# A new order table for the fused attention and MoE kernel, and other numbers of attention units per token chunk

## The chip, the cores and the metric

The kernel runs on one core of one Trainium2 chip. Its time is the device time of one execution in microseconds, the median of several runs. The core has five instruction queues: TensorE (PE in the profile, with its weight loads as PEld), VectorE (DVE), ScalarE (ACT), GpSimd (POOL) and SyncE (SP). In this kernel POOL and SP carry no arithmetic worth speaking of: POOL issues the loads from memory, SP issues the stores and the transposes by DMA.

## The reference

Sliding-window attention with a distance bias, then a two-layer MoE block with a cosine gate:

```python
# q, k, v: (8, 8, 576, 64)
scores = scale * q @ k^T
bias = slopes[:, None, None] * (-np.abs(rel))
mask = (rel >= 0) & (rel < 128)
scores = np.where(mask, scores + bias, -1e9)
attn = softmax(scores)
x = (attn @ v).transpose(0, 2, 1, 3).reshape(4608, 512)
h = x @ w_in             # (4608, 2048)
g = h * np.cos(h)
out = g @ w_out          # (4608, 512)
```

## The kernel before

**Attention.** A batch has nine *units*: for each half of its first 512 tokens (`G` = 0, 1) four pairs of heads, and one tail unit `t` with the last 64 tokens of all heads. Units are taken two at a time. Each pair goes through a chain that changes engine at every step:

- `scores` (PE, L497, the tail L488): keys times queries into four PSUM banks. These matmuls use 64 rows of the array, all others 128.
- `exps` (ACT, L529, tail L521), then `mask` (DVE, L553, tail L540), which multiplies by the precomputed bias and window `emask`.
- `pv` (PE, L584 and L587, tail L571 and L573): probabilities times `vp`; a column of ones in `vp` gives the sum.
- `norm` (DVE, L623 and L625, tail L610 and L613): reciprocal and product. Where the two units of a pair are neighbours of the same half and the count of units so far is even, `norm_two` (L638 and L640) does both at once.
- The result is turned into `xT`, either by PE (`x_pe`, L691, copied by L700 on ACT or L701 on DVE; `x_pe_two`, L653 and L664), or by a DMA transpose that SP issues (`x_dma`, L714, tail L709) where there is time.

**MoE.** Tokens are cut into nine chunks of 512. `moe1` (chunk 0: `moe1_half`, L753, L758, L762) makes 16 *feature blocks* per chunk: four matmuls of L729 into one bank, the cosine on ACT (L735), the product `gT` on DVE (L739). The bank comes free when DVE has finished. `moe2` multiplies `gT` with `w_out`: plainly for chunk 0 (`moe2_plain`, L814, L820, L826), and for the others with seven products of Strassen's scheme (L870), sums made by DVE (`g_sums`, L804), reads by ACT (L890) and DVE (L894), stores by SP (L915).

**Which units stand beside which chunk.** Batch 0 is done ahead of the loop. Beside chunk `c` stand the next `QUOTA[c]` units (L272, used in L1018). Their chain fills the waiting times of MoE work and the other way round.

**Loads.** POOL issues, in program order: the pieces of q and k for batches 0 and 1 (L309), the weights `w_inb` (L360) and `w_outb` (L366), `vp` by `load_v` (L328, five per batch, two buffers by `b % 2`), and from batch 2 on q and k in natural layout by `load_nat` (L338). `load_v` reads the key `("vinit", b % 2)`: it waits for DVE's memsets of that buffer (L393 and L394). From batch 2 on SP transposes q and k by DMA (`dma_transposes`, L349 and L352) into `qt` and `kt`, which `scores` reads.

**Order.** `Plan.op` records every step with what it reads and writes. `Plan.schedule` does not search: it decodes the string `STARTS` into a 16-bit number for every step. The upper 15 bits are a start number, the lowest bit picks DVE or ACT for steps that may run on either. Steps are sorted by start number, and each engine gets its own steps in that order:

```python
            code = (code + 256 * raw[i] + raw[n + i]) & 0xFFFF
            o.start = code >> 1
            if len(o.eng) > 1:
                e = "dve" if code & 1 else "act"
...
        self.order = sorted(self.all, key=lambda o: (o.start, o.seq))
```

The start numbers themselves are not on the chip. `Plan.emit` puts semaphore waits where a step's data or buffer comes from another engine or from a DMA; a queue is strictly in order, so a step that waits holds all steps behind it on its engine. POOL's steps keep program order whatever the table says.

Of the kernel before, what the change touches and what calls it, by code (L numbers as in the profile page):

```python
# [14 lines left out]
B, H, S, D = 8, 8, 576, 64  # L15
# [12 lines left out]


STARTS = (  # L30
    "c-p;I4^&iD8lM5w+uPIjylD=XA&1L@)!DZ=!DE==&YKwm#u0JCBtYD7mURWuZ3#Cu{8JK=x<ux>u7#<cUH{g))KN}(j+SLb="
    "&I{6D{HsS&X)FPv&{tL&+K<+U>Fz>t8@09^WNP1-S7VSe&6r+-O*@$J(|9!uhpaVX*8odd>UV%3k|Km<KwSJ)7K1nq9P)@uL"
    "MRknm(tV{xt&zU!Oy8d|+1#zgn%PBkV-Mg-2{@hOqVA;CeSY+8we<r#3R^(-%g6-xty!7_)ESnr;5xs7Or&$3W9QI>M*DJUF"
    "6J?Sm~*or4UKn!!HWknQ_6^o4}c9byUh8SdLN7<OL>NWr!*1iFC%kGd8(ZkP5doDeea>(UOJzpw=KJ`p`5x`eMXx@|B(+Hg>"
    "MIBx#7HZ<FVvo@k7gc-hpx){V5txwxOldEkY-2NYa&WNtixxhZZTs7J@f1UwF&38sI{0VdE%~mMS!YrsG3`JiMzoAgP5nO#k"
    "(ait$1Pzf<SA%D03nsW1?$Mgip0=kmq8G6CfK}W5-O-5b8qp<8mzvR6ud{G}fL%kD8*O;u8Dj1a8r2R>m|j{!x_!Ovi0+V*&"
    "Y>977BX#g=eMJ{GP|$!7M@P+|A&x6#OE7I*4H8A^+h~P-P80FGJp^?BZAo<!)X@KY%c{PB0ECojryjShh5(Tgw7FN#)RD%H("
    "lu~dy##n&LM@X`3}PE9wr;17a{*fb#?b^xL<mmP=lcp+4eoO*gY~2dTzkd5mNR;Gab-g;M)_%fMG1!fd4?o@DR1yjuAr)OKQ"
    "}}A!={n-qTzi=HP*#`wo7+5H;7e0Jr(c!Y*ZB@Vvt--8V#3K5b`6yb=Dt3E^w_hOy;M@O?gkO4R>cPESlU=x$H{P;S@lYI2t"
    "Ddc^H^y4`h^$)7~kAHigf?{cxWO;@zz8OO%wzjivEwsiP_hugiz*6faRmFXwn{zy%nn*4_0(Fa%7I;FYtM|3y2H%&S#PM`j4"  # L40
    "aRgoZS2}mDLpqBy5?-Ek$o61k>B?DFv0b_)=_)O#IC|x$tCwtxzb_H#5fac^^-lu)ib7H?dr3eTA&i|Y7Ev=n0x=afA}=47^"
    "lZF<L~xaLES4aN&(*837-kTJ2zwM!FSLj`b1|5N1JbLdQ;!OKOh7tz(7&=E61EcwZYt!~>K=%}9)xXtv{2;3m6GoLGDScxO5"
    "{m1;v5NE7LLs~dvoWVp6`9(MC)=Q>hH)9FM484Ul{k#Z{2AY$*iB@tN9(XJ|`vn)_#>cI}L(NB_G5+tIYE?6gtF<%2=WyFG|"
    "1KbXVFqns9=Hc<G(d4d=YPHTK}o6TKU#OT^Wpl&%!u+eC~FmU>)+MWsZPptlQ)PWrIPDfZB<ISLld*p1I+B_^N6L@#0yJ4>*"
    "rrw58RxbvwZO6=FzB~n(1vALc-w7!}e*xq9o*5^3V<huX9sQ!W$87WIqJk-S2;bqEm>OEAUiRuE*4aZOB!<RiFiG;FKN)4W*"
    "9<8Eck~&_bGG&W5o8vua^$$&vGAAFD&3}>C&tIIK&Jt2qHE(a7V-+0<>ymTcYB-gK)r60vxALYyz%vCN<}%BcwSTvmkDRyYv"
    "mSGjN)M8G!V&-IE+-2Wi04obZ?ayAUKbogL=WjC?ybD1mwSx@ihYphmougoC8AYGm}tGghp1jaOOTw1>hf6XQvz~=EeZUJIL"
    "+2=F95tKJBURI0>j(zddHK-eNjrr-@J=(3457r!<*SH7~6^*zr$iVRUK5yDp2Dw#Yw7KMMM)TGrF*aO{bU`?rGdgFlCRI5F2"
    "Hyxev=e-SUj_kXd~Ict0cNXi}?e9-C7{=B5BA64FnSx{W)g8^>~n+(aVCwx*gNEqmMA+mlT>sU+9<a+)H&<4vHfRyN14*O?Q"
    "5UBzEo_8)TBx(}?-c^kb-i6y;6v-~qsX(yF3M+C!5jujwOArMRg7$wKOg@P~=&=X2bUICb;3*tDx=s*e+8~vk+V!3RVP?3P5"  # L50
    "?>GX2;wu)@9Y`LxLRhZdh>@9tE#;c{(o*WgL%0`3Y+$?LTd&T>`Bet>%VdgAI%ek=U^Dv|?D>v|M64+6BOtMveF_NO$^Hly%"
    "2Htko4Ot7ouux@P>?bngVazq26RBx<xiQ_+|x@_oGo|%o-F%7$w}M1J;U8@zhgzc**()#IWt9kx;_m{OV1fCH@7yJKjc;Coq"
    "5GZOIp)8vN{bU_nP+$3bc!=ZuLI@>K0SEWkW@LkW+z=&Hxy=poJ;W%!7pJ!#FS~1D+BuDd(F4=(;%3cr)g8?or^8?0g;=vNO"
    ";4nTb#lTHAoARJHQ$0wg6TfwcjXq`Eg0Dcbr83RE5glpv#o2u753V~d}{_3U+V$qG!}r|nPg-0YM96YxtA@&t<9l7YP@LX}f"
    "&pvSpz1{rD@WeWgMqfD@2>0U$yqdy&UAr8KWtnS4|B9~(^ku~zIU=KrPp>RNeVOT{?szP8h(#&jyvjWz0WN)iHwIkE2oE06e"
    "^DCOSpIG`!`hr+?q`{PP7x}0DJu8;1mnY)!cB3=(Wci*sQ$)S^aqFHl?h3c7c(*r;<GX+MIG3&3BNBlGP$c_Y=|U|D;w{E}C"
    "4{B`3%4gf>~CT?rGFNh_!5T%Rbr_1z&gPa9r+(*@=qW*Ij1#$3re-Zv9nA_vY|U6ym@lslhy_R4J4>=3QdzmslM#ZL(Mp!t+"
    "c<3J&wjnM9ez86lmtLE=a~8-$q_z*&0qf_8WdBvT2G7gx*%fS2*aW<s}i98`yh(&*@t%H|L6FDeG5Rb{b0BS2Z7RPH{lZ{dE"
    "7kN={7as>l>Nxl7eaR-0_TzxD<4_)KM=F}6}NTE_qOPCMiDbUd~4T1&1z-E{5i0W1WZfQL4yY=m<JqQcP!1E_GZAqjBN-IwG"
    "in;lpPWs;zA(U0@KOsWXM0xtm>$31*GjP<$r908WhTX4(WVi7RhLgc*W5`hXh+FC(5Q)W;XmeqAoyXx8Wrc&I+RxdKv)v1dW"  # L60
    "C69t|jV?fiDlS9gH*o#rs8cAlORSATft$M6WmBru$&^ZlsW*85z!`7a0KbJk!tb1!7n`>?zvMWRc%<y)DkW#l>DMxN=q`_R@"
    "5A>4iDqSc8x~boUD$W&{6!)m*~qib8LE3VP>^_d$VN>lW~#us+l!Jc6LR+^4v~>8A%r;j#UH&|Ksms7<U)3G&0cL>XuU#+M}"
    "{7%GQtm%qpf@73uG&)LY1(S;u5M;tuUR`&zPW)&6JhNn>>bDPudAE;Oh&;GR>awuXElCHLitvC#h>hSGALUD^aD1sT*4Wi8;"
    "&6HpB4;yq;y0EtCPLF~>y{Xf&m!N|6c=*X(yCF~z&-jMH*V+AYW)MC2BQQ=14Sq+CGWEU#TOKUeh`AvS&V^EH2l_$VzRHU%Q"
    "Xx|6bG<Pztoh#2?~x3U1@hssQlELKZ0er(z+e%4UIFI{+JthWhN){Bx~IG`jU+M0LXm9;CAmBYQxrqS|(MaSQ#MO!J0%-U+8"
    "RwyW+(YT|usm8$m0b4h)y_HG<EsMp9r}XeCdjTXelI+Jxj`0PrxD1ZM0_vepWVo=AX8*xM?FRL<w{}tW7SoR}QP3$4FqNOGC"
    "2uVz<P#T0&LVF`E0$?W-mMZ`1Q-|D6`ov0Z=@%b1A(-{faI-!W~6SGl2=h*wWoFigk3LdXlHzP{4p5jbL+V`k#Kav`w69h2G"
    "mEi$A6&-=+^ju$Nvukga^0"
)


# [150 lines left out]
def bass_alibi_sliding__then__act_gcu_kernel(  # L222
# [8 lines left out]
    with ExitStack() as ctx:  # L231
        def sb(name, shape, dt=BF16):
            return ctx.enter_context(nc.sbuf_tensor(name, shape, dt))

        R = Plan(nc, ctx)
# [8 lines left out]
        T = {n: sb(f"wsum{n}", [128, HF, 256], F16) for n in (1, 2, 3, 4)}  # L244
# [9 lines left out]
        P = [sb(f"p{i}", [128, 2, 512]) for i in range(NP)]  # L254
# [14 lines left out]

        ps = ctx.enter_context(nc.psum_tensor("ps", [128, 8, 512], F32))  # L270
        BPE = 2
        QUOTA = [9, 9, 12, 10, 8, 10, 5]  # L272
        SB, UB, OB = [4, 5, 6, 7], [2, 3], [0, 1]

        slopes = [2.0 ** (-8.0 * (h + 1) / H) for h in range(H)]
# [508 lines left out]
        NG = 2  # L784
# [220 lines left out]
        for c in range(NCH):  # L1005
# [8 lines left out]
            else:  # L1014
                for fc in range(NFC):
                    moe1(c, fc, (UB + SB)[fc % 6] if done < len(every) else
                         (UB + SB)[(16 * c + fc) % 6])
            n = QUOTA[c] if c < len(QUOTA) else 0  # L1018
            attention(every[done:done + n], c)
# [40 lines left out]
```

The softmax here doesn't subtract the row's maximum and nothing guards it: scores larger than these inputs give would overflow.

## Time and profile before

| | |
|---|---|
| median of 4 runs | 305.56 us (305.48 to 305.7) |
| the profiled execution | 305.43 us, of which the span of instructions is 303.7 us |
| PE busy | 293.9 us, 97% of the span |
| DVE, ACT, POOL busy | 252.0 us (83%), 203.9 us (67%), 94.9 us (31%) |
| mean granted TensorE clock | 0.994 of full speed |
| MoE1 matmuls (L729), busy | 125.9 us |
| MoE2 products (L870), four groups, busy | 46.8, 46.1, 43.7 and 26.3 us |
| loads by POOL, median from issue to landing | `qnat` 9.0, `knat` 13.1, `w_outb` 21.4, `vp` 7.7 us |
| transposes by SP, median to landing | `qt` 6.9, `kt` 8.5 us |

A line of the waits says who waited for whom: engine, tile and line, then the total in us, the number of times and the longest. A line of the timeline has the start and the length in us, the engine, the line, the operation, the tile written and read, the number of instructions, and in brackets the idle time ahead and what ended it. Matmuls are pipelined: a record runs from a matmul's start to the end of its last result, so the records of matmuls that follow one another overlap.

### The profile page before, as it was taken

To read this page: it belongs to the slowest core of one execution; us is meant where nothing else is said; L and a number is where in the kernel's file an instruction comes from. 1 tells how busy PE (TensorE), PEld (TensorE's weight loads), DVE (VectorE), ACT (ScalarE), POOL (GpSimd) and SP (SyncE) were. 2 spreads that over 40 slices of the span, in tenths; PEclk is the share of its full clock that TensorE was granted. 3 is DMA by queue.
4 is the path that set the end of the run, shared out by engine and by line. 5 is a ranking of instruction groups with operands and counts; after the bars stand their busy time and mean duration, and the time that the engine had idled before them with its cause. 6 is when DMAs were issued, how large, how long until landed. Compare 5 with 4: busy or idle time off the path is not lost.

```text
span 303.7 us, 7149 instructions
## 1 busy us (share of the span) xinstructions
PE 293.9 (97%) x2893; PEld 197.7 (65%) x2911; DVE 252.0 (83%) x542; ACT 203.9 (67%) x293; POOL 94.9 (31%) x122
## 2 busy tenths in 40 slices
PE   8699999998999999999999999999999999999996
PEld 3478745546874587537888886468646765555785
DVE  3788758789888998989988988999988976788963
ACT  6796877688556787797757875778667935556211
POOL 7998240053998701860188004000000000000000
PEclk9889999999999999999999999999999999999999
DMA  7999999999999999999899989960120314010044
GB/s 144 181 203 210 207 164 155 131 190 123 163 192 156 156 173 178 149 162 165 101 166 149 165 108 108 174 136 15 25 69 4 95 28 143 14 35 0 2 139 140
DMA packets 148353, 38.09 MB, mean 125 GB/s; under 512 B 133984, under 2 KB 147040, under 8 KB 148320
## 3 DMA queue, kind: packets, MB, share of 16 engines
q0 software_dynamic: 99344, 18.10, 80.0%
q1 hardware_dynamic: 48976, 19.54, 33.3%
q8 instruction: 23, 0.38, 0.5%
q14 instruction: 10, 0.08, 0.1%
HBM read 36.70 MB, written 9.44 MB: 152 GB/s over the span
## 4 chain that ended last, share of the span: by engine, by line
PE 89%; DMA 4%; DVE 3%; SPq 2%; ACT 1%; issue 1%; DVEq 0%
PE ps L870 32%; PE ps L729 32%; PE ps L497 5%; PE ps L814 5%; PE ps L753 5%; PE ps L584 3%; DMA kt<-knat 2%; PE ps L587 2%; SPq L349 2%; PE ps L442 1%; DMA ob<-in_q_dram 1%; PE ps L691 1%; PE ps L488 1%; DVE p L553 1%; PE ps L571 1%
## 5 line engine op out<-in xcount | busy, mean ns | idle before, releaser
L729 PE MATMUL ps<-xT,w_inb 128*128 128x512 bf16 (+1 forms) x558 | 125.9, 355 | 0.9 <-issue 0.2
L735 ACT ACTIVATE cos<-ps,halfpi 128x512 f32<-128x512 f32 x128 | 83.0, 686 | 46.1 <-PE ps L729 33.0
L739 DVE TENSOR_TENSOR gT<-ps,cos 128x512 f16<-128x512 f32 x128 | 83.1, 686 | 15.2 <-ACT cos L735 14.4
L729 PEld LDWEIGHTS ps<-xT,w_inb 128*128 128x128 bf16 x576 | 54.5, 98 | 44.5 <-DVE gT L739 5.9
L529 ACT ACTIVATE p<-ps 128x768 bf16<-128x768 f32 (+1 forms) x64 | 56.3, 917 | 14.8 <-PE ps L497 12.6
L328 POOL DMA_DIRECT2D vp<-in_v_dram x40 | 33.9, 887 | 64.4 <-PE ps L587 53.5
L870 PE MATMUL ps<-wsum,gT 128*128 128x256 f16 x256 | 46.8, 273 | 0.1
L870 PE MATMUL ps<-wsum,gsum 128*128 128x256 f16 x256 | 46.1, 273 | 0.1
L553 DVE TENSOR_TENSOR p<-p,emask 128x512 bf16<-128x512 bf16 (+2 forms) x96 | 42.0, 460 | 3.9 <-ACT p L529 3.4
L870 PE MATMUL ps<-w_outb,gT 128*128 128x256 f16 x256 | 43.7, 273 | 0.1
L338 POOL DMA_DIRECT2D qnat<-in_q_dram x30 | 25.6, 908 | 17.7 <-DMA qt<-qnat 16.5
L870 PEld LDWEIGHTS ps<-w_outb,gT 128*128 128x128 f16 x256 | 25.0, 98 | 7.3 <-DVE ob L894 0.3
L338 POOL DMA_DIRECT2D knat<-in_k_dram x30 | 25.6, 924 | 10.0 <-DMA kt<-knat 8.3
L870 PEld LDWEIGHTS ps<-wsum,gT 128*128 128x128 f16 x256 | 23.7, 98 | 6.1 <-DVE krows L894 0.3
L870 PEld LDWEIGHTS ps<-wsum,gsum 128*128 128x128 f16 x256 | 23.4, 98 | 6.3 <-issue 0.8
L870 PE MATMUL ps<-w_outb,gsum 128*128 128x256 f16 x128 | 26.3, 273 | 0.1
L625 DVE TENSOR_TENSOR xnat<-ps,rec 128x256 bf16<-128x256 f32 x56 | 22.0, 419 | 0.5
L497 PE MATMUL ps<-qt,kt 64*128 64x128 bf16 (+1 forms) x320 | 19.2, 245 | 2.0 <-DVE kt L460 1.1
L584 PEld LDWEIGHTS ps<-vp,p 128*128 128x128 bf16 x256 | 16.2, 98 | 6.7 <-issue 4.0
L584 PE MATMUL ps<-vp,p 128*128 128x65 bf16 x256 | 18.4, 195 | 1.9 <-DVE p L553 1.8
L497 PEld LDWEIGHTS ps<-qt,kt 64*128 64x128 bf16 x320 | 11.4, 96 | 10.1 <-ACT p L529 3.0
L587 PE MATMUL ps<-vp,p 128*128 128x65 bf16 x192 | 17.3, 194 | 0.0
(78 smaller groups left out, 334.5 us busy)
## 6 DMA issues: line engine op xcount, KB each, us to landing
out_dram<-ob SPq DMA_DIRECT2D x32, 256.0 KB, 2.8
vp<-in_v_dram POOLq DMA_DIRECT2D x32, 128.0 KB, 7.7
qnat<-in_q_dram POOLq DMA_DIRECT2D x24, 128.0 KB, 9.0
knat<-in_k_dram POOLq DMA_DIRECT2D x24, 128.0 KB, 13.1
w_inb<-in_moe_w_in_dram POOLq DMA_DIRECT2D x4, 512.0 KB, 9.9
w_outb<-in_moe_w_out_dram POOLq DMA_DIRECT2D x4, 512.0 KB, 21.4
out_dram<-ob SPq DMA_DIRECT2D x8, 128.0 KB, 1.8
qrows<-in_q_dram POOLq DMA_DIRECT2D x1, 576.0 KB, 14.8
```

What stands on the lines that cost most here:

```text
L328: op("pool", [lambda e, t=t, rows=rows: e.dma_start(vp[b % 2][0:rows, t, :, 0:64], v[b, :, 128 * t:128 * t + rows, :].rearrange("h p d -> ...
L338: fns.append(lambda e, t=t, rows=rows: e.dma_start(nat[which][b % 2][0:rows, t, :, :], src[b, :, 128 * t:128 * t + rows, :].rearrange("h p ...
L497: ins = e.matmul(ps[:, banks[x], c0:c1], keys_ap(b, x, pr, kc), query_ap(b, x, pr, qb, 128 * nb), start=True, stop=True)
L529: op("act", lambda e: e.activation(P[i][:, :, 0:hi], src_[:, :, 0:hi], ACTF.Exp, scale=0.125), w=held + [("P", i)], occ=920 if G else 691, ...
L553: op("dve", lambda e, p=p, m=m: e.tensor_tensor(p, p, m, ALU.mult), r=[("P", i), ("EM", h0), ("EM", h1)], w=[("P", i)] if n != 1 else [("P ...
L584: ins = e.matmul(o, P[i][:, x, d0:d0 + 128], V[:, kc, h, 0:65], start=True, stop=not two)
L587: ins = e.matmul(o, P[i][:, x, p0:p0 + 128], V[:, kc - 1, h, 0:65], start=False, stop=True)
L625: op("dve", lambda e: e.tensor_tensor(o, U[:, :, :, 0:64], rv[:, :, :, None].broadcast_to([128, 2, 2, 64]), ALU.mult), r=[("rec", n % 2)], ...
L729: op("pe", lambda e, kc=kc, c0=c0: e.matmul(ps[:, bank, c0:c0 + n], w_in[:, kc, 128 * fc:128 * fc + 128], xT[:, kc, (r0 + c0) % XR:(r0 + c ...
L735: op("act", lambda e: e.activation(cosb[ci][:, :], ps[:, bank, :], ACTF.Sin, bias=halfpi[:, 0:1]), r=["halfpi"], w=[("B", bank), ("cos", c ...
L739: op("dve", lambda e: e.tensor_tensor(gT[gi][:, fc, :], ps[:, bank, :], cosb[ci][:, :], ALU.mult), r=[("cos", ci)], w=[("B", bank), ("g", ...
L870: op("pe", lambda e, t=t, fc=fc, bk=bk: e.matmul(ps[:, bk, 256 * t:256 * t + 256], lhs(fc, t), rhs(fc), start=first and fc == 0 and (last ...
```

## The change

The diff has two parts. Nothing else differs; no step's work or cost in the code is altered.

```diff
-        QUOTA = [9, 9, 12, 10, 8, 10, 5]
+        QUOTA = [9, 9, 11, 10, 10, 9, 5]
...
 STARTS = (
-    "c-p;I4^&iD8lM5w+uPIjylD=XA&1L@)!DZ=!DE==&YKwm#u0JCBtYD7mURWuZ3#Cu{8JK=x<ux>u7#<cUH{g))KN}(j+SLb="
...
+    "c-pmA4^&iD8lN|)U7v2}_PNP$8F9Qks2!igp(iuUn?Im1jmQ~56cABI)@Vdpk@TcUs6^%=#6M9h9=9mTGOO)$(%fpvZEIIa4"
...
```

The string is a new table. Decoded as in `schedule`, it says the following.

*Units and counts.* Chunk 2 has 11 units for 12, chunk 4 has 10 for 8, chunk 5 has 9 for 10. The pairs of batches 4 to 7 are therefore cut differently, more of them are neighbours of one half:

| step | before | after |
|---|---|---|
| `scores` steps on PE | 42 | 43 |
| `norm` of one unit, tails aside (two DVE instructions each) | 56 | 36 |
| `norm_two` (two DVE instructions each) | 4 | 14 |
| `x_pe` and `x_pe_two` on PE | 26 and 4 | 25 and 5 |
| `x_dma` on SP | 38 | 37 |
| evictions of q and k of batches 0 and 1: ACT, DVE | 10, 6 | 8, 8 |
| `xT` copies: ACT, DVE | 20, 10 | 19, 11 |
| all DVE instructions of the plan | 542 | 525 |

*SP's queue from the first transposes on.*

```
before                          after
x_dma tail of batch 0           x_dma tail of batch 0
qt of batch 2 (L349, L352)      qt of batch 2
x_dma tail of batch 1           kt of batch 2
store, store, store (chunk 0)   store, store (chunk 0)
kt of batch 2                   x_dma tail of batch 1
store (chunk 0)                 store, store (chunk 0)
qt of batch 3                   qt of batch 3
store, store (chunk 1)          kt of batch 3
kt of batch 3                   x_dma tail of batch 2, store (chunk 1)
```

*DVE at the start, from the first eviction of batch 0's second piece on.* Before: `qt` eviction; one mask of the second unit; both masks of the first unit; `kt` eviction; further masks. After: both masks of the first unit; `qt` eviction; both masks of the second unit; `kt` eviction; further masks. The memsets of `vp` for odd batches (L393, L394) stand before the first `kt` evictions in the old order; in the new one L393 follows the first two `gT` of chunk 0, and L394 comes nine `gT` steps later, shortly before the norm of batch 0's tail. Two `xT` copies of batch 0 stand ahead of, and between, the masks of its fifth and sixth unit in the new order; in the old one they come after these two.

*PE around the end of batch 3* (number of matmuls of MoE work between successive attention steps):

| between | before | after |
|---|---|---|
| `pv` of units 4, 5 and the first x transpose | 7 of L870 | 9 of L870 |
| that and the next x transpose | 1 of L870 | 2 of L870 |
| `pv` of units 6, 7 and their first x transpose | 8 of L870 | 5 of L870, 2 of L729 |
| the last `scores` and the tail's `pv` | none | 3 of L729 |

*PE ahead of batch 2's first `scores`* stand three matmuls of the second product of chunk 1 in the new order, one in the old.

*Least distance in start numbers* between a step and the one that uses its result, in steps of the table's grid (the last start number is 11877 before and 11873 after): from `gT` (L739) to the next matmul in its bank 30 before and 36 after; from `norm` to the MoE1 matmul in its bank 21 and 24; from the last product of `mask` to `pv` the same in both, 17.

## The prediction

> **What bounds the kernel now.** I read the page first, then the chain of waits, PE's own waits, the SP and PE timelines, and tables of windows.
>
> ```profile
> PE 293.9 (97%) x2893; PEld 197.7 (65%) x2911; DVE 252.0 (83%) x542; ACT 203.9 (67%) x293; POOL 94.9 (31%) x122
> ```
>
> PE is the bound: 293.9 of 303.7 us. The diff takes no matrix work away, so it can only change PE's stops. Idle time alone undercounts them: in the groups by line a 256-column matmul of L870 has a mean of 273 ns, but in the PE timeline such matmuls start 0.109 us apart, so a stop under 0.16 us shows as no idle and a longer one shows 0.16 us too short. PE's waits:
>
> ```profile
> PE ps L584 <- DVE p L553: 1.8, 2, 1.6
> PE ps L415 <- DVE p L412: 1.3, 1, 1.3
> PE ps L497 <- DVE kt L460: 1.1, 1, 1.1
> PE ps L497 <- DMA kt<-knat: 0.8, 1, 0.8
> ```
>
> The first three lie before 14 us. The fourth is one stop at 73 us; the chain passes through it, and SP's timeline tells why (start, duration, instruction):
>
> ```profile
> 48.87 5.10 SPq L349 DMA_TRANSPOSE qt<-qnat  x1
> 54.00 1.25 SPq L352 DMA_TRANSPOSE qt<-qnat  x1
> 59.02 1.17 SPq L709 DMA_TRANSPOSE xT<-xtail  x1
> 60.24 1.54 SPq L826 DMA_DIRECT2D out_dram<-ob  x3
> 61.83 4.67 SPq L349 DMA_TRANSPOSE kt<-knat  x1
> ```
>
> SP is free from 55.25 us, but the next entry of its queue, the transpose of batch 1's tail, waits until 59.02 for VectorE, three stores follow, and only then is batch 2's key transpose issued. It lands at about 73.4 us (the chain's DMA piece starts at 66.53 and lasts 6.82). In PE's timeline:
>
> ```profile
> 72.36 0.27 PE L870 MATMUL ps<-wsum,gsum 128*128 128x256 f16 x1
> 73.40 0.50 PE L497 MATMUL ps<-qt,kt 64*128 64x256 bf16 x8 [0.77 <-DMA kt<-knat]
> ```
>
> Windows show two more stretches (length; PE, PEld, DVE, ACT and POOL busy; PEclk):
>
> ```profile
> 6.65:10.07 3.42, 2.30 (x46) 1.35 (x42) 1.94 (x6) 2.68 (x6) 3.42 (x6) 1.00 1.38 183
> 10.07:13.48 3.41, 1.77 (x44) 1.32 (x42) 3.34 (x10) 3.16 (x5) 3.41 (x6) 1.00 1.62 192
> 13.48:16.89 3.41, 3.23 (x42) 2.32 (x40) 3.06 (x12) 2.56 (x3) 3.41 (x6) 0.50 1.99 177
> ...
> 117.00:124.00 7.00, 6.53 (x110) 4.63 (x110) 5.61 (x18) 5.60 (x10) 1.87 (x3) 1.00 1.80 175
> ```
>
> The start is latency-bound on DVE and ACT (3.34 and 3.16 of 3.41 us), and after the stretch with 1.77 us of PE work the clock is halved for 3.41 us. At 117 to 124 PE loses 0.47 us visibly.
>
> **The change, part by part.** The table gives only order and the choice of ACT or DVE, so I compare what stands between a producer and its consumer.
>
> *Keys of batch 2.* L349/L352 for the keys move up behind those for the queries, ahead of one tail transpose and two stores. They can issue at 55.25 instead of 61.83, 6.58 us earlier; the keys' own load landed at 52.8 in this trace. From issue to landing they took 73.4 − 61.83 = 11.6 us, so 66.9 us, against a need at about 72.8 (without its wait the score would start at 72.63, and two more L870 matmuls now stand ahead of it). Slack 5.9 us, so the stop goes: −0.8 us (0.77 idle and a little hidden). Bounds: −0.9, and 0 if the transposes share the engines badly. Late next are only the tail's tokens, first read by MoE1 of chunk 2 near 89 us, some 20 us later, and the two stores, whose buffers chunk 1 refills around 80.
>
> *117 to 124 us.* Here PE passes the end of batch 3 and waits on VectorE at step after step. By start-to-start gaps beyond the steady 0.109: 118.67 to 118.99 loses 0.21, 119.11 to 119.32 and 121.41 to 121.62 lose 0.10 each, the P·V before them (117.54) about 0.2, and the tail's P·V about 0.3 behind DVE's mask (L540 runs until 122.68, the matmul starts at 122.83): 0.9 us. In the new order nine products instead of seven stand ahead of the first of these transposes (+0.22 us of PE work against the 0.21 lost), two instead of one ahead of the second (+0.11 against 0.10), five products and two matmuls of L729 instead of eight products ahead of the third (0.98 instead of 0.87, +0.11 against 0.10), and three matmuls of L729 instead of nothing ahead of the tail's P·V (+0.65 against 0.3). That covers 0.21 + 0.10 + 0.10 + 0.3, so I take −0.7; bounds −1.0 and, since DVE is 80% busy there (5.61 of 7.00), +0.3.
>
> *Bank hand-overs in MoE1.* PEld waits for gT before 133.76 and 136.13 by 0.38 and 0.53 us where its neighbours wait 0.27, and before 159.24 PE waits for xnat (PE idle 0.14, with the hidden part 0.30): 0.37 + 0.30 = 0.67 us. In the new table the least distance from gT to the matmul that reuses its bank is 36 grid steps for 30, from xnat 24 for 21; with 11,877 steps over some 300 us a step is 0.025 us, so 0.15 and 0.075 us of room more. I take −0.5; bounds −0.7 and 0.
>
> *VectorE's load.* Ten more pairs of units are normalised by L638/L640 (204 + 687 = 0.89 us) instead of twice L623/L625 (2 × (169 + 419) = 1.18): 10 × 0.29 = 2.9 us less DVE work, beside PE's own work, so 0 on the path. If PE were not covered by MoE it would be worth what a stop before P·V is worth, so it backs the −0.7. Two `kt`/`qt` evictions (about 0.8 us each) and, on balance, one `xT` copy go to VectorE from ScalarE, all before 60 us, where DVE was about 80% busy: also 0.
>
> *One more `scores` step* (43 for 42). Around 105.69 the switch to 64-row matmuls costs 105.69 − 105.38 − 0.11 = 0.20 us and the way back 0.12; no matmul is added. +0.3 us, bounds +0.2 and +0.4.
>
> *POOL's queue.* The memset of `vp` for odd batches (L394, 0.27 us) moves from 7.41 to about 32 us on DVE. L328 for batch 1 waits for it, and behind it stand L338 for q and k of batch 2 and L328 for batch 2, so POOL issues from about 33 instead of 17.28. I cost it at nothing: batch 2's query load was issued by 25.7 us and still held SP until 48.87, because w_out, issued ahead of it, lands only at 40.7; the DMA queue and not the issue sets the landing. Four L328 (4.2), five L338 twice (8.5) from 33 us end at 46, before 52.8. If that cover is gone, see the first rival.
>
> *The start.* VectorE now does both masks of the first unit before the second query eviction, and the memset is gone, so the first P·V (12.69 now, 1.73 us after the last score's start of 10.78 with its 0.18 us of work) can come some 0.3 us earlier. On the other hand the first P·V of the second token half waits for two `xT` copies that now stand ahead of its masks on DVE, and PE then has no MoE1 block left until a bank comes free (about 0.8 us). I take −0.2. Bounds: −1.1 if the clock stays full (at half clock eight x transposes took 1.03 us, at 56 ns each they take 0.55; twelve scores 1.04 against 0.55; P·V 0.15: 1.1), and +1.7 if a second stretch is halved (3.41 × 0.5).
>
> The clock, by the rows: 2.30 of 3.42 us busy kept it, 1.77 of 3.41 lost it; the longest hole in that stretch was 1.7 us. The Trainium skill, in "TensorE: Matmul & The Clock Gate", section "Why this matters for your kernels", tells to avoid idle gaps over about 3 µs; by it the halving would not have come at all, and no hole of the new order could bring one. This trace disagrees. By the rule the sum would stand without the +1.7 bound; I keep it.
>
> *New misses.* No order is free of them. The old one lost 0.77 + 0.9 + 0.67 = 2.3 us after 20 us; I let the new one lose a sixth of it, +0.4, bounds 0 and +1.5.
>
> Sum: −0.8 − 0.7 − 0.5 + 0.3 − 0.2 + 0.4 = −1.5 us. The profiled execution took 305.43 us (span 303.7), so 303.9; the median of the runs, 305.56, lies 0.13 above it: 304.1 us.
>
> **The rivals.** *POOL holds up the keys (slower).* If batch 2's key load lands later than 72.8 − 11.6 = 61.2 us, PE stops at batch 2's first scores. For it: POOL starts 15.5 us later. Against it: the backlog above; by issue at 46 and the page's median of 13.1 us to landing it is 59.1, close. Were the whole 15.5 us carried on, landing at 68.3 gives keys at 79.9, a stop of 7.1 us: about 311. A middling case (landing at 63.5) gives keys at 75.1, a stop of 2.3: 304.1 + 2.3 = 306.4. Chance 0.14.
>
> *The clock is halved a second time,* at about 20 us, because of the hole after the early P·V. Price 1.7 in place of −0.2: 306.0, no difference to be measured. Chance 0.10: 16.89 to 20.30 now has 3.13 us of PE work, and losing 1 us leaves 2.1, between the two rows.
>
> *The stops only move:* VectorE is 83% busy, and after each P·V it is late somewhere else. Then only the keys' 0.8 and the score's 0.3 remain: 305.56 − 0.5 = 305.1, from 304.6 to 306. Chance 0.16.
>
> *The clock stays full at the start:* 0.9 better than the forecast, 303.2. Chance 0.10.
>
> **How the numbers follow.** The forecast, 303.2 to 305 by its own bounds, has the remaining 0.50. About 0.2% or 0.6 us can be told from no change, so faster means under 304.95 and slower over 306.17. Faster: 0.50 + 0.10 + half of 0.16 = 0.68. Same: the other half, the second halving, less a little for spill over: 0.17. Slower: 0.14 and 0.01 of the second halving, 0.15. The range 302.5 to 306.3 leaves out most of the first rival and a twentieth below.
>
> **What would show it.** Right: SP issues L349 `kt` within 1 us of the end of L352 `qt` near 55 us; PE's wait for `kt<-knat` is gone; POOL's L328 of batch 1 starts near 33 us with SP's `qt` transpose still near 49; PE idle at batch 3's tail under 0.2 us; L640 runs 14 times; PE's busy time about the same and its span near 302.2 us. Wrong: SP's first `qt` transpose well after 50 us, PEclk below 1 after 17 us, or a new row of PE waits above 0.5 us after 20 us.

## The result and the profile after

The new order took 303.58 us (median of 50 runs, 302.11 to 305.21) against 304.9 us for the old one beside it (74 runs): a ratio of 0.9955, 95% interval 0.9945 to 0.9964. It is 1.3 us faster. The forecast was 304.1 us and 1.5 us faster. The profiled execution took 304.23 us and its span is 302.2 us, the span that was forecast. Behind the table the lines stand one lower than before (L729 is L728, L870 is L869).

The page's busy row, and TensorE's own waits (line, what it waited for, total us, times, longest):

```profile
PE 291.1 (96%) x2893; PEld 198.9 (66%) x2913; DVE 252.5 (84%) x525; ACT 203.2 (67%) x290; POOL 95.0 (31%) x122
```

```profile
PE ps L583 <- DMA vp<-in_v_dram: 1.6, 2, 0.9
PE ps L752 <- DMA w_inb<-in_moe_w_in_dram: 1.3, 2, 0.9
PE ps L414 <- DVE p L411: 1.3, 1, 1.3
PE ps L496 <- ACT kt L458: 0.9, 1, 0.9
...
PE ps L583 <- DVE p L552: 0.5, 1, 0.5
PE ps L869 <- ACT ob L889: 0.3, 1, 0.3
```

The wait for `kt<-knat` is gone. Three rows are new: two waits for loads before 25 us (`vp`, `w_inb`), and one for an eviction into `ob`, of which more below. SP's timeline and TensorE's at the place of the old wait:

```profile
51.72 4.98 SPq L348 DMA_TRANSPOSE qt<-qnat  x1
56.74 1.25 SPq L351 DMA_TRANSPOSE qt<-qnat  x1
58.04 4.86 SPq L348 DMA_TRANSPOSE kt<-knat  x1
62.94 1.25 SPq L351 DMA_TRANSPOSE kt<-knat  x1
```

```profile
73.69 0.38 PE L869 MATMUL ps<-wsum,gsum 128*128 128x256 f16 x2
74.00 0.50 PE L496 MATMUL ps<-qt,kt 64*128 64x256 bf16 x8
```

The keys go out 0.05 us behind the queries, land at 65.3 us, and the scores start at 74.00 with no idle time ahead of them. The windows of the start and of batch 3's end:

```profile
6.65:10.07 3.42, 1.97 (x34) 1.00 (x34) 1.67 (x5) 3.29 (x7) 3.42 (x5) 1.00 1.39 192
10.07:13.48 3.41, 2.19 (x48) 1.56 (x48) 3.25 (x11) 3.17 (x5) 3.41 (x6) 1.00 1.58 176
13.48:16.89 3.41, 2.75 (x52) 1.91 (x53) 3.38 (x13) 3.41 (x6) 3.41 (x5) 1.00 1.92 177
16.89:20.30 3.41, 2.01 (x30) 1.40 (x28) 1.92 (x7) 3.22 (x4) 0.85 (x2) 1.00 1.33 203
...
117.00:124.00 7.00, 6.93 (x106) 4.87 (x106) 5.36 (x17) 5.68 (x10) 1.96 (x3) 1.00 1.83 218
```

The clock is full throughout (it was 0.50 from 13.48 to 16.89 before), although TensorE does less work at the start. Between 117 and 124 us it is busy for 6.93 of 7.00 us, before for 6.53.

**Where the time went.** Idle time undercounts TensorE's stops, so I use another measure: how late a matmul starts against its own start number in the order table, at 0.025 us a step. What this lateness grows by in a stretch is what the stretch loses. A stop that the table itself plans for does not show in it. The stretches are bounded by scores steps that stand at the same place in both orders. All values are us, from one profile each; rows and sum are rounded one by one.

| stretch | before | after |
|---|---|---|
| start to the first scores of batch 1 (near 40) | 1.27 | 2.46 |
| from there to the first scores of batch 2 (near 73) | 1.08 | 0.02 |
| to the last pair of units of batch 3 (near 115) | 0.29 | 0.38 |
| to 139 (the end of batch 3) | 0.70 | 0.11 |
| to the last scores (near 240) | 1.00 | 0.44 |
| to the end of the span | 2.44 | 2.01 |
| sum | 6.78 | 5.41 |

The two tables end 4 steps (0.10 us) apart, so 1.37 + 0.10 is the 1.5 us between the spans. A P·V that starts at 125.39 us in both profiles splits the fourth stretch: ahead of it the old order loses 0.47 us and the new one 0.14, behind it the old one 0.22 and the new one nothing. In the fifth stretch the largest single loss of the old order is 0.32 us at 159 us. Five profiles of the old order and nine of the new (these two and those of the experiments below) repeat a stretch to 0.07 us, mostly to 0.02, where neither the edit nor the landing of a DMA touches it. The first row, and in the new order the third, differ from one execution to the next.

### The profile page after: what moved, and what is told of

Read it like the earlier page. It is cut to its first block, busy times and chain, and to the rows that moved or that the text cites. A ratio compares the mean times of both kernels' runs of the same rounds, so it can differ in the third digit from the quotient of the medians.

```text
span 302.2 us, 7119 instructions
## 1 busy us (share of the span) xinstructions
PE 291.1 (96%) x2893; PEld 198.9 (66%) x2913; DVE 252.5 (84%) x525; ACT 203.2 (67%) x290; POOL 95.0 (31%) x122
## 4 chain that ended last, share of the span: by engine, by line
PE 64%; DMA 18%; POOL 9%; SPq 4%; ACT 1%; issue 1%; DVE 1%; ACTq 0%
PE ps L869 28%; PE ps L728 27%; DMA qnat<-in_q_dram 8%; POOL vp L327 4%; SPq L348 4%; POOL qnat L337 4%; DMA w_inb<-in_moe_w_in_dram 4%; PE ps L496 3%; DMA out_dram<-ob 2%; DMA qt<-qnat 2%; PE ps L752 2%; PE ps L583 2%; DMA ob<-in_q_dram 1%; POOL knat L337 1%; PE ps L586 1%
## 5 line engine op out<-in xcount | busy, mean ns | idle before, releaser
L728 PE MATMUL ps<-xT,w_inb 128*128 128x512 bf16 (+1 forms) x556 | 126.9, 354 | 0.7
L728 PEld LDWEIGHTS ps<-xT,w_inb 128*128 128x128 bf16 x576 | 55.0, 98 | 39.1 <-DVE xnat L624 0.7
L869 PE MATMUL ps<-wsum,gT 128*128 128x256 f16 x256 | 44.8, 273 | 0.1
L869 PE MATMUL ps<-wsum,gsum 128*128 128x256 f16 x256 | 42.8, 273 | 0.3 <-ACT ob L889 0.3
L869 PE MATMUL ps<-w_outb,gT 128*128 128x256 f16 x256 | 42.6, 273 | 0.1
L869 PEld LDWEIGHTS ps<-w_outb,gT 128*128 128x128 f16 x256 | 25.0, 98 | 8.7 <-DVE ob L893 0.3
L869 PEld LDWEIGHTS ps<-wsum,gsum 128*128 128x128 f16 x256 | 24.3, 98 | 7.2 <-ACT ob L889 0.6
L869 PEld LDWEIGHTS ps<-wsum,gT 128*128 128x128 f16 x256 | 24.0, 98 | 5.6 <-issue 0.5
L869 PE MATMUL ps<-w_outb,gsum 128*128 128x256 f16 x128 | 27.1, 273 | 0.1
L752 PE MATMUL ps<-xT,w_inb 128*128 128x256 bf16 x128 | 16.2, 273 | 1.3 <-DMA w_inb<-in_moe_w_in_dram 1.3
L813 PE MATMUL ps<-w_outb,gT 128*128 128x512 f16 x64 | 16.8, 380 | 0.0
## 6 DMA issues: line engine op xcount, KB each, us to landing
w_inb<-in_moe_w_in_dram POOLq DMA_DIRECT2D x4, 512.0 KB, 11.5
```

What stands on the lines that cost most here:

```text
L728: op("pe", lambda e, kc=kc, c0=c0: e.matmul(ps[:, bank, c0:c0 + n], w_in[:, kc, 128 * fc:128 * fc + 128], xT[:, kc, (r0 + c0) % XR:(r0 + c ...
L752: op("pe", lambda e, i=i, fc=fc, kc=kc: e.matmul(ps[:, bank, 256 * i:256 * i + 256], w_in[:, kc, 128 * fc:128 * fc + 128], xT[:, kc, r0:r0 ...
L869: op("pe", lambda e, t=t, fc=fc, bk=bk: e.matmul(ps[:, bk, 256 * t:256 * t + 256], lhs(fc, t), rhs(fc), start=first and fc == 0 and (last ...
```

## The experiments

Each kernel was profiled and timed beside runs of the old order. A ratio is to those. "Old" and "new" are the kernels before and after. The edits sort steps anew by changing start numbers in `Plan.schedule`; `trq0` and `trk0` are batch 2's transposes, `xt1` batch 1's tail, `st0` the store of output buffer 0, `trk1` batch 3's keys. Times below that are not from a ratio come from one profile.

**1. Keys early in the old order.**

```diff
+        q2 = next(o for o in self.all if o.dma == "trq0")
+        k2 = next(o for o in self.all if o.dma == "trk0")
+        k2.start = q2.start + 1
```

> The kernel before, with one entry of SP's queue moved: the key transposes of batch 2 follow those of the queries at once, as in the changed kernel; nothing else. Theory (the stop at batch 2's first scores was SP's order): the keys' transpose is issued within 1 us of 56 us, PE's wait for kt<-knat (0.77 us) is gone, and the time falls by 0.8 us (0.5 to 1.0) against the kernel before. Rival (the two transposes share the DMA engines, so the keys land as late as before): the wait stays within 0.3 us of 0.77 and the time is unchanged.

Measured: 304.52 us, ratio 0.9983 (0.9965 to 1.0000), span 302.8. SP and TensorE:

```profile
54.01 1.25 SPq L355 DMA_TRANSPOSE qt<-qnat  x1
55.31 5.13 SPq L352 DMA_TRANSPOSE kt<-knat  x1
...
72.50 0.51 PE L500 MATMUL ps<-qt,kt 64*128 64x256 bf16 x8
```

The scores start at 72.50 instead of 73.40, with no wait. The lateness gained between 40 and 73 us falls from 1.08 to 0.30; no other stretch after 40 us moves by more than 0.02. So this one move of SP's queue is worth 0.78 us in the trace. The runs give half of that: 0.35 us in the medians, with an interval that just reaches no change, and 0.4 us in the means of executions with the same granted clock (304.08 against 304.47 us at 0.999 and above, 304.68 against 305.10 us at 0.993 and 0.994). Why they gain less than the profile was not found.

**2. Keys late in the new order.**

```diff
+        x1 = next(o for o in self.all if o.dma == "xt1")
+        k2 = next(o for o in self.all if o.dma == "trk0")
+        k2.start = x1.start + 1
```

> The changed kernel with that one entry put back: the key transposes of batch 2 stand behind the transpose of batch 1's tail again. Theory: PE waits at batch 2's first scores again, by 0.5 to 2 us (this start-up is later or earlier by up to 1 us from run to run), and some 0.8 us of the gain are lost: about 0.5 us faster than before in place of 1.3. Rival (in the new order the DMA queues are emptier there): no wait, and the time stays that of the changed kernel.

Measured: 304.82 us, ratio 1.0011 (0.9981 to 1.0041), span 302.5. SP, and the one wait that is larger than in the new order:

```profile
61.58 3.17 SPq L351 DMA_TRANSPOSE kt<-knat  x1
64.79 1.25 SPq L354 DMA_TRANSPOSE kt<-knat  x1
```

```profile
PE ps L872 <- ACT ob L892: 1.2, 1, 1.2
```

Here the keys go out at 61.58 us, as late as in the old order (61.83), and yet nothing waits for them: they land after 7.9 us, at 69.5, where the old order needed 11.5. In the old trace POOL's loads of batch 3's queries were issued at 61.09, ahead of the keys; here at 63.71, behind them. That this traffic is the reason was not tried by itself. The early issue is thus enough to end the wait (experiment 1), but in the new order it was not needed to. What the kernel loses lies elsewhere: at 110 us, 1.33 us in the third stretch.

**3. The store at 110 us.** In the new order SP issues chunk 1's store from `ob` buffer 0 behind batch 4's query transposes, which wait for their load; the old order issued it at about 84 us, ahead of batch 3's keys. The new order's SP, ACT and TensorE:

```profile
101.58 1.30 SPq L351 DMA_TRANSPOSE qt<-qnat  x1
102.92 0.59 SPq L914 DMA_DIRECT2D out_dram<-ob  x1
...
109.84 0.60 ACT L889 ACTIVATE ob<-ps 128x512 f32<-128x512 f32 x1 [0.62 <-DMA out_dram<-ob]
...
110.50 0.83 PE L869 MATMUL ps<-wsum,gsum 128*128 128x256 f16 x6 [0.26 <-ACT ob L889]
```

The store lands at 109.82 us; only then may ACT evict chunk 2's result into the same buffer and free TensorE's bank. The loss in the third stretch was 0.38 us in this profile and 0.09 to 1.33 in others of the new order that leave the store alone. In three of the four profiles with an untouched store in which batch 1's scores start before 40.5 us it was above 1.1: an early TensorE only waits longer for SP. The edit puts the store back ahead of the queries:

```diff
+        st = [o for o in self.all if o.dma == "st0"][1]
+        k3 = next(o for o in self.all if o.dma == "trk1")
+        st.start = k3.start + 1
```

> The changed kernel with one entry of SP's queue moved: the first store of chunk 1 (out buffer 0) goes right behind batch 3's key transposes instead of behind batch 4's query transposes. In the changed kernel's trace it is issued at 102.92, after a transpose that waits for its own load until 95.39, and ACT waits for that store's landing (0.62 us at 109.84), and PE behind it. New theory (a cost that the forecast put at nothing): the store is issued near 89 us, ACT's wait for out_dram<-ob and PE's wait for ACT ob at 110 us go, and 0.35 us and more are gained over the changed kernel, up to 1.2 (as much as PE lost there in the two other kernels with this order): about 1.7 to 2.2 us faster than before. Rival (the wait hides a stop that comes anyway a step later): the wait goes, the time stays.

Measured: 302.8 us, ratio 0.9936 (0.9906 to 0.9966), span 301.2.

```profile
87.97 1.10 SPq L917 DMA_DIRECT2D out_dram<-ob  x1
...
108.61 0.60 ACT L892 ACTIVATE ob<-ps 128x512 f32<-128x512 f32 x1
...
109.43 0.83 PE L872 MATMUL ps<-wsum,gsum 128*128 128x256 f16 x6
```

Both waits are gone and the stretch loses 0.05 us. The median is 0.8 us below the new order's, though the two intervals overlap; at a granted clock of 0.999 and above the means are 302.85 and 303.38 us.

**4. The end of batch 3 without its cover.** The three MoE1 matmuls ahead of the tail's P·V go behind it:

```diff
+        for o in self.all:
+            if o.eng[0] == "pe" and o.pri == 5 and 4805 < o.start < 4834:
+                o.start = 4835
```

> The changed kernel with the three matmuls of MoE1 that stand between the last scores of chunk 2 and the P.V of batch 3's tail moved behind that P.V. Theory (the gain at the end of batch 3 comes from work in PE's queue that covers the wait on VectorE's mask): PE stops there for 0.2 to 0.5 us behind the mask of ptail, and that much is lost over the changed kernel. Rival (VectorE is simply earlier there, because of the other cut of units): PE stops for under 0.1 us and nothing is lost.

Measured: 304.19 us, ratio 0.9975 (0.9951 to 1.0000), span 302.1. First the two rows of TensorE in the new order, then those of this kernel:

```profile
123.12 0.82 PE L728 MATMUL ps<-xT,w_inb 128*128 128x512 bf16 x3
123.83 0.19 PE L570 MATMUL ps<-vp,ptail 128*128 128x65 bf16 x1
```

```profile
122.08 0.34 PE L499 MATMUL ps<-qt,kt 64*128 64x256 bf16 x4
123.06 0.19 PE L573 MATMUL ps<-vp,ptail 128*128 128x65 bf16 x1 [0.65 <-DVE ptail L542]
```

The stop is there with 0.65 us; the fourth stretch loses 0.76 us instead of 0.11, and no later stretch gives it back. The median moves by 0.6 us. So in the new order this cover is needed. It does not follow that the old order lost as much here. At the tail's P·V it stood idle for only 0.16 us:

```profile
122.83 0.19 PE L571 MATMUL ps<-vp,ptail 128*128 128x65 bf16 x1 [0.16 <-DVE ptail L540]
```

**5. Less room at the hand-overs of `gT`.** One memset of a single column ahead of each of the 128 products that write `gT` is to delay them on VectorE; the same edit in both orders:

```diff
+            def late(e, ci_=ccount[0] - 17):
+                e.memset(spare[:, ci_:ci_ + 1], 0.0)
+                return e.tensor_tensor(gT[gi][:, fc, :], ps[:, bank, :], cosb[ci][:, :],
+                                       ALU.mult)
```

> The kernel before with one more DVE instruction of about 60 ns, a memset of one column that nobody reads, ahead of each of the 128 gT products of chunks 1 to 8: every hand-over from gT to PE and every DVE queue is 60 ns later. Theory (PE stops where the distance to VectorE is too short): the old order has as little as 58 ns of room over its own latency, so many hand-overs turn into stops: 2 to 5 us slower than before. Rival (PE is busy with other work and the distances do not matter): under 1 us.

> The changed kernel with the same added DVE instructions. Theory: with 75 to 150 ns more room per hand-over it loses at most half of what the old order loses by them: 0.5 to 2 us over the changed kernel, so it stands to the kernel before at about the same time, and its lead over the old order with the same load grows from 1.3 to over 2.5 us. Rival (the gain has nothing to do with room, only with the keys of batch 2 and the end of batch 3): both lose the same, and the lead stays at 1.3 us.

Measured: old 305.01 us, ratio 1.0007 (0.9990 to 1.0024); new 303.73, ratio 0.9962 (0.9941 to 0.9984). A memset takes 59 ns, but 128 of them raise VectorE's busy time only from 252.0 to 252.4 us in the old order: they mostly overlap their neighbours. A product's record even starts ahead of that of its memset:

```profile
157.66 0.69 DVE L742 TENSOR_TENSOR gT<-ps,cos 128x512 f16<-128x512 f32 x1
157.69 0.06 DVE L741 MEMSET spare<- 128x1 f32 x1
```

At the earliest a product starts 30 ns behind the end of its cosine in the old order and 40 ns behind it with the memset: the load is some 10 ns a product, not the 60 ns that were expected. Nothing followed from so small a load, so I tried three of them at each place.

> The kernel before with three memsets of one column (59 ns each as measured, so some 0.18 us) ahead of each of the 128 multiplications that write gT: a stronger form of the 60 ns run, which changed nothing. Theory that the old order has too little room in these hand-overs: it loses at least 0.5 us more than the new order does under the same load; 306 to 309, ratio 1.004 to 1.013. Rival: VectorE takes the 23 us in its idle time (252 of 303.7 us busy), and what is lost is the same in both orders.

> The same three memsets in the kernel after. Theory of more room: it loses less than 0.5 us against its own 303.6, ratio at most 0.998, and its lead over the kernel before with the same load grows from 1.3 to at least 1.8 us. Rival: both lose the same and the lead stays at 1.3 us, within the 0.5 us that such runs differ by; if after loses more, the new order has less room at this hand-over and not more.

Measured: old 306.15 us, ratio 1.0046 (1.0022 to 1.0070); new 303.99, ratio 0.9974 (0.9958 to 0.9989). The groups by line show what was added, in the old order:

```profile
L742 DVE MEMSET spare<- 128x1 bf16 x384 | 9.7, 59 | 0.0
```

The lead of the medians grows from 1.3 to 2.2 us. From 40 us on the old order's lateness grows by 1.33 us more than without the load (6.84 to 5.51), the new one's by 0.51 (3.46 to 2.95). This says less than it seems. By the same measure three memsets delay a product by 26 ns (56 for 30), not by 0.18 us. The profiled executions are the second slowest (306.97 us) and the fastest (303.27 us) of their twelve. And at a granted clock of 0.999 and above the old order loses 0.8 us (305.30 us, mean of 4, against 304.47), the new one 0.7 us (304.11, mean of 12, against 303.38).

Where the load costs time says more. Behind the P·V near 125 us, up to 139 us, it costs the old order 0.22 us and the new one nothing; this is where the forecast's first two waits for `gT` lie. From there to 240 us it costs the old order 0.17 us and the new one 0.40. So more room is shown at the first place only, and after 139 us the new order has no more of it than the old. The waits of TensorE's weight loads (PEld) for `gT`, first before and then after the change, fit the first part:

```profile
PEld ps L729 <- DVE gT L739: 5.9, 21, 0.5
```

```profile
PEld ps L728 <- DVE gT L738: 0.2, 1, 0.2
```

**6. The joint normalisation undone.** The new cut makes 14 pairs share one reciprocal and one product (`norm_two`), the old one 4. Here each is done as two of each:

```diff
-            op("dve", lambda e: e.reciprocal(rv, U[:, :, :, 64]),
+            def recs(e):
+                for u in range(2):
+                    ins = e.reciprocal(rv[:, u, :], U[:, u, :, 64])
+                return ins
...
+                    ins = e.tensor_tensor(
+                        o[:, u, :, :], U[:, u, :, 0:64],
+                        rv[:, u, :, None].broadcast_to([128, 4, 64]), ALU.mult)
```

> The changed kernel with each of the 14 joint normalisations done by two reciprocals and two products of half the size, as the single ones do it: about 0.3 us more VectorE work for each, 14 x 0.29 = 4.1 us in all, nothing else. Theory (VectorE's work lies beside PE's): under 0.4 us lost. Rival (the gain came from the lighter VectorE queue): 1 us or more of the gain goes, and new PE waits for xnat appear.

Measured: 304.04 us, ratio 0.9967 (0.9943 to 0.9992), span 302.2. The groups of VectorE, first of the new order, then of this kernel (count, then busy and mean ns):

```profile
L639 DVE TENSOR_TENSOR xnat<-ps,rec 128x512 bf16<-128x512 f32 x14 | 9.7, 690 | 0.4
...
L637 DVE RECIPROCAL rec<-ps 128x8 f32<-128x8 f32 x14 | 2.9, 204 | 2.2 <-PE ps L586 2.2
```

```profile
L644 DVE TENSOR_TENSOR xnat<-ps,rec 128x256 bf16<-128x256 f32 x28 | 10.6, 418 | 0.4
...
L639 DVE RECIPROCAL rec<-ps 128x4 f32<-128x4 f32 x28 | 3.5, 165 | 2.3 <-PE ps L586 2.1
```

A pair now takes 2 × (418 + 165) = 1166 ns instead of 894. No row of the matmuls' waits shows it; those of the weight loads do, first in the new order, then in this kernel:

```profile
PEld ps L652 <- DVE xnat L639: 0.3, 1, 0.3
PEld ps L583 <- DVE xnat L639: 0.3, 1, 0.3
```

```profile
PEld ps L662 <- DVE xnat L644: 0.9, 3, 0.4
PEld ps L583 <- DVE xnat L644: 0.6, 2, 0.4
```

The stretch up to 115 us, where this run loses hardly anything to the store, loses 0.41 us instead of 0.05 (the value with the store early), and the stretch to 240 us loses 0.89 instead of 0.44. That is 0.8 us in the trace; the median moves by 0.5 us, inside the interval. The two parts differ in what they say of the change. The first part, some 0.35 us, belongs to the four pairs of batch 2, joined at 80 to 90 us, and the old order joins these four as well. The ten pairs that only the new order joins lie between 146 and 219 us, in the stretch that loses 0.45 us.

**7. The start.** In the new order the memsets of the value buffer for odd batches come at 34 us, so POOL's loads behind them do too:

```profile
34.59 4.20 POOL L327 DMA_DIRECT2D vp<-in_v_dram  x5 [16.85 <-DVE vp L393]
```

Experiment: these memsets early in the new order.

```diff
+        for o, s in zip([o for o in self.all if ("vinit", 1) in o.w], (205, 288)):
+            o.start = s
```

> The changed kernel with the two memsets of vp for odd batches put back to the start of VectorE's queue, as before the change. Theory (the DMA queue, not POOL's issue, sets when these loads land): POOL issues batch 1's vp from about 18 us instead of 34.6, the keys of batch 2 land within 2 us of where they landed (55.2), SP's transposes start within 2 us, and the time is that of the changed kernel within 0.3 us. Rival (POOL's late start delays the loads): SP's first transposes start 3 us and more earlier; or the memsets' 0.36 us on VectorE show as a later first P.V and 0.3 us are lost.

Measured: 303.16 us, ratio 0.9941 (0.9917 to 0.9964), span 301.3. Batch 1's first scores start at 39.48 us instead of 41.18, and the first `w_in` piece lands at 14.6 us, as in the old order, and not at 16.0. By then POOL had not yet come to the step that the edit frees, so I asked whether it was the edit at all: once with both edits in the new order, once with the late memsets (and POOL's loads behind them) in the old one.

> The kernel after with two of its steps moved: the second store of the first chunk right behind batch 3's key transposes, and the two memsets of the second value buffer back to the starts they have in the kernel before. Theory: these are two separate losses, so the gains add. The wait of L889's eviction for the store is worth 0.35 us in the profile of after (1.2 in that of the kernel with the early memsets alone), the late landing of the first weights about 1.3: span 302.2 - 0.35 - 1.3 = 300.5, time 302.0 to 302.9, ratio 0.990 to 0.993; the first w_in lands at 14.3 to 14.8 us, no wait of TensorE for ob near 110. Rival: the landing of the first weights differs from one execution to the next and has nothing to do with the memsets: it is then as likely at 15.5 to 16.3, and the time is that of the early store alone, 302.8, ratio 0.9935.

> The kernel before with the memsets of the second value buffer, and all that follows them in the load queue up to 1400, at the starts they have in the kernel after (552 units of 25 ns later in the table). Theory that the late memset costs the start: the first w_in lands at 15.5 to 16.3 us instead of 14.3 to 14.8, the first scores of batch 1 start about 1 us later, time 305.6 to 306.3, ratio 1.002 to 1.005. Rival A: the landing does not follow the memset; 14.3 to 14.8 us and 304.7 to 305.2. Rival B, that of the prediction: the later loads of batch 2 hold up the transposes of its queries and keys; the first query transpose then starts past 52 us and the wait of the first scores of batch 2 for kt grows from 0.8 us by the same amount, up to 2 us in the time.

(The "second store of the first chunk" in the text on record is the store of experiment 3.) Measured: both edits in the new order 302.9 us, ratio 0.993 (0.991 to 0.995), first `w_in` at 16.4 us, first scores at 41.10. Old order with late memsets 304.91, ratio 0.9995 (0.9975 to 1.0016), first `w_in` at 14.8 us, first scores at 39.87; batch 2's wait for its keys is 0.9 us against 0.8. Both refute the memset theory: the early landing in the first kernel was not the edit's doing. For the prediction's rival the last kernel is the direct test, and it speaks against it: POOL's late start alone costs no time.

What is left is a pattern without a cause. The first `w_in` piece, issued near 8 us in every kernel, landed at 14.3 to 14.8 us in all five profiles of the old order, and at 15.5 to 16.4 in eight of nine of the new (14.6 in the ninth). The first scores of batch 1 started at 39.8 to 40.2 us (mean 40.0) and at 39.5 to 41.2 (mean 40.4). The landing alone does not set that start: in the new order with one and with three memsets of experiment 5 it came at 15.8 and 15.7 us, and batch 1 started at 40.0 and 39.8. In the new order the memory traffic is lower from 11 to 13 us (179 and 181 GB/s in the profiled execution against 205 and 207 in the old). What in the new order lowers it was not found.

The best version is the one with the store early, with or without the memsets: 302.8 and 302.9 us, 2.1 to 2.3 us below the old order's 305.0 to 305.1 beside them.

## Why the prediction was right, and where it was not

The forecast of 1.5 us holds: 1.3 in the medians, 1.5 in the spans. Its sum holds partly because errors cancel: the start, priced at −0.2, cost 1.2 us in the profiled pair, and gains that nothing had priced stand against it (0.4 us at the end, 0.2 us near 52 us). That the span came out as forecast is in part luck.

- **Keys of batch 2, −0.8.** Right: SP issued them 0.05 us behind the queries, the wait is gone, and the move alone is worth 0.78 us in the old order's trace and 0.4 us in its runs. What fell short is "late next": in the new order the keys would have been in time anyway, because the 11.5 us from issue to landing are not a constant: with another order's traffic around them they were 7.9. In the profiled pair the stretch gained 1.06 us, 0.2 of it near 52 us from another cause.
- **117 to 124 us, −0.7.** Right in kind, about twice too large: the window's idle time fell by 0.40 us, and of the 0.59 us in the table's fourth stretch 0.34 lie ahead of 125.39 us. Taking the three matmuls away costs 0.65 us at the place that was named, which shows the cover at work, though the old order had stood idle there for only 0.16 us.
- **Bank hand-overs, −0.5.** The size is about right, and so are the places: the two waits for `gT` lie behind 125.39 us, where the old order loses 0.22 us and the new one nothing, and the stop at 159 us (0.32 us of lateness) is gone. Experiment 5 shows more room between 125 and 139 us. For the stop at 159 us no run tells the distance in the table from the other changes.
- **VectorE's load, 0.** This is the step that failed. The prediction found 2.9 us less work by ten more joint normalisations and costed it at nothing, because it lies beside TensorE's work. Undoing all 14 costs 0.8 us, but some 0.35 of that at four pairs that both orders join. The ten others cost 0.45 us, so zero was too low by up to that much. This and the stop at 159 us cannot be added up: together they exceed the 0.56 us that the stretch gained in all, and the new order has a stop of its own there (0.16 us at the P·V at 155.96 us). Whether the work on VectorE counts, or only that each pair ends later, the runs do not separate.
- **One more scores step, +0.3.** It cannot be read off: both tables have it in their numbers, and they end 0.10 us apart in the new one's favour.
- **POOL's queue, 0.** Right in the sum, and the first rival is refuted (experiment 7). One of the signs for it did show: the first query transpose started at 51.72 us, not near 49. Its load had landed only then. The cover held: the keys landed at 65.3 us and were needed at 74.0.
- **The start, −0.2.** Wrong in both halves. The clock was kept, as the last rival had it: in 41 of 50 runs of the new order the granted clock was 0.999 or above, in 24 of 99 of the old one beside the experiments. That rival's number, 303.2 us, is nearer to the result than the forecast's 304.1. But the profiled start was 1.2 us later, not earlier, by the waits for `vp` and `w_inb` in the rows above; the one for `w_inb` that ended at 21.75 us, 0.85 us long, is a sign that the prediction had named for being wrong. At equal clock the new order is ahead by 0.7 us (304.41 against 305.07, means at 0.994) to 1.1 us (303.38 against 304.47, at 0.999 and above). The rest of the medians' lead comes from the clock being kept more often.
- **New misses, +0.4.** Right in size, and the store at 110 us is one of them. The prediction followed only chunk 0's stores to their reader. Chunk 1's store of buffer 0, the second of the two that the list of SP's queue shows ahead of batch 3's keys for the old order, moved to behind batch 4's queries, where the list for the new order has already ended; it was costed at nothing because it was not looked at.
- **The end.** The last 60 us gained 0.4 us (2.44 to 2.01), and no step of the prediction dealt with them. I did not look for the reason.

On the clock, the rule of the Trainium skill ("TensorE: Matmul & The Clock Gate", "Why this matters for your kernels") was right about the new order and wrong about the old. The share of work in a stretch, by which the prediction went instead, does not tell the two apart either. The halved 3.41 us begin at another time in each execution (at 12.73 to 14.90 us in the five profiles of the old order), so the stretch to look at is the one ahead of them. In experiment 1 it held 2.00 of 3.41 us of work and the clock was lost. With the store early (experiment 3) the clock was kept after 1.97 of 3.42 us, in a stretch counted in the same steps of 3.41 us from where that trace's record of the clock begins:

```profile
11.49:14.90 3.41, 2.00 (x42) 1.35 (x40) 3.33 (x14) 2.71 (x5) 3.41 (x6) 1.00 1.57 191
14.90:18.31 3.41, 3.41 (x53) 2.70 (x54) 2.77 (x7) 3.41 (x6) 3.41 (x6) 0.50 1.70 189
```

```profile
17.64:21.06 3.42, 1.97 (x29) 1.26 (x28) 2.65 (x8) 3.36 (x5) 0.53 (x1) 1.00 1.26 207
21.06:24.47 3.41, 3.41 (x47) 3.12 (x45) 2.44 (x9) 1.44 (x3) 0.00 (x0) 1.00 1.25 210
```

What decides it was not found.

## What to carry to other kernels

When a step moves in an in-order queue, list every step that it passes and every step that lands behind a new waiter, and follow each to the reader of its buffer: here a store that nobody needed soon became late because a transpose ahead of it waits for a load. On a path that is full to 96%, a shorter step on the next busy engine can be worth something even where no wait of the matmuls names it; look at the waits of the weight loads too, and measure by the start times against the order's own numbers, which repeated within 0.07 us between profiles. Before crediting a difference between two orders to a feature, check where it stands in each: four of the 14 joint normalisations were in both. Before explaining a shift in the start by an edit, look at the same start in other profiles: one early landing of a load looked like the effect of a memset and was not.

## What was not expected of the hardware

- The granted clock was kept with 1.97, 2.19, 2.75 and 2.01 us of TensorE work in four stretches of about 3.4 us, in an order that does less work there than the one that lost it; in experiment 1 it was lost after 2.00 of 3.41 us.
- A key transpose by DMA took 11.5 us from issue to landing in the old order, 7.3 in the new one and 7.9 in the new one with the late issue, for the same bytes.
- One load of 512 KB, issued at 7.6 to 8.4 us, landed between 14.3 and 16.4 us; it went with the kernel's order in 13 of 14 profiles, and the reason is open.
- A 59 ns memset ahead of each of 128 products added 0.4 us to VectorE's busy time, where 128 × 59 ns would be 7.6, and delayed a product by some 10 ns.
